# Chunk-selected attention with a gated linear unit: fp16 keys and queries spread by DMA, two gate taps on GpSimd, fewer constants loaded

## The chip, the cores and the metric

The kernel runs on one core of a Trainium2 chip. The metric is device time in microseconds (us) of one execution of the whole kernel. The engines are named as in the profile: PE (TensorE; PEld is its weight load), DVE (VectorE), ACT (ScalarE), POOL (GpSimd) and SP (SyncE, which here issues DMAs). "L793" is line 793 of the kernel before.

## The reference

There are 4 batches with 8 heads, 768 positions and 64 columns per head, all fp32. Keys are cut into 24 chunks of 32 positions. For each query an upper bound of its score with every chunk is formed from the chunk's minimum and maximum; the six chunks with the highest bound are kept, and ordinary causal softmax attention runs on those alone. The result, 512 columns wide, then goes through a gated linear unit: a causal convolution of five taps per column gives a gate, a matmul with `w_val` gives a value, and their product is multiplied with `w_out`.

```
k_min, k_max = min and max of k over each chunk of 32
ub   = sum(maximum(q*k_min, q*k_max))          # future chunks: -1e9
top  = the 6 chunks with the highest ub
attn = softmax(q k^T / 8, only chunks in top, only positions j <= i)
x    = attn v                                  # heads side by side: 512 columns
gate = sigmoid(sum over 5 taps of conv_w[t] * x[s-4+t])
out  = (gate * (x w_val)) w_out
```

## The kernel before

The work is cut into 16 pairs of heads; four pairs (512 columns) make a batch. Everything for a pair has two heads in the upper and lower 64 partitions.

`load` issues the DMAs of a pair's keys, queries and values (`kn`, `qn`, `vn`, positions on partitions) on SP, and for pair 0 on ACT's queue too. `kq(p)` turns keys and queries round with fp32 transposes on PE (L548) into PSUM banks. ACT copies them to SBUF as fp32 (`k32` L559, `q32` L581) and makes the rectified queries `rq` (L586). DVE takes minima and maxima of the chunks (L565). POOL casts each head's half into the fp16 score operands `KE` and `QU` (L573, L592, four casts of 64x384 each), casts values into `VA` (L636), and, from pair 2 on, builds the bound operand `KB` (L607, L614). There are three `KE`/`QU`/`VA` buffers, so pair p writes the buffer that pair p-3 used.

`sel(p)` makes the choice: matmuls of `rq` and `q32` with `KB` (L664) give the bounds, DVE adds a loaded table `cfill` that marks future chunks (L671, into SBUF tile `mub`), takes the eight highest per query (L680), compares with the sixth (L687) and writes the mark `NS`. PE transposes it (L697). For pairs 0 and 1 ACT and DVE copy one head's half each into the spare rows of `QU` (L720); from pair 2 on ACT copies all to `t_m` (L711) and two DMAs on SP carry the halves (L715). Rows of `KE` with a constant -240 per chunk (table `echunk`) make the score matmul itself add the penalty.

`attn(p)` works on 11 banks of scores: score matmuls (L793), the exponential on ACT (L800, `t_P`), a triangular select on POOL where a bank holds diagonal blocks (L807), value matmuls with a column of ones (L824). DVE divides by the sum (L750, L754). A DMA transpose puts the result into `xT`, columns on partitions (L766); the last pair uses PE and ACT (L775, L780).

`moe_gate` makes the gate of a pair's 128 columns in two halves of 384 positions. The first tap, split into two fp16 parts, is a PE matmul with a diagonal (L850); taps 2 to 5 are DVE instructions that add to the PSUM bank (L859). In the last batch the third pair has three taps and the fourth all five on PE. The diagonals are built at the start by DVE (L931). ACT takes a tanh (L863). `moe_val` (L874, L881) and `moe_out` (L890, L896 or L900, output DMA L903) finish a batch.

The order of work on each engine is written by a planner (`class Plan`). Each operation is added with a cost, a due time (`key`, moved by a table `SHIFT` per kind of operation), what it reads and writes, and buffers or PSUM banks that it needs (`CAPS`, `BUFS`). `order` walks through modelled time and picks, for each engine, the ready operation that is due first. Where PE would idle, it puts in warm-up matmuls on a tile of zeros (`filler`, L530). The result is a fixed sequence for each engine's queue, in which an instruction that waits holds back all behind it. `warm_rows` (L507) is a fixed burst of warm-up matmuls at the start.

Of the kernel before, what the change touches and what calls it, by code (L numbers as in the profile page):

```python
# [9 lines left out]
FP = mybir.dt.float32  # L10
# [6 lines left out]
class Op:  # L17
    __slots__ = ("eng", "key", "cost", "fn", "kind", "reads", "writes", "new", "need", "ndep",
                 "outs", "after", "ready", "end", "num", "at")


class Plan:
# [18 lines left out]
    def add(self, eng, key, cost, fn, r=(), w=(), new=(), kind=None, at=0.0):  # L41
# [6 lines left out]
        key = round(key + self.shift.get(eng + ":" + what, 0.0), 4)  # L48
        o.eng, o.key, o.cost, o.fn, o.kind, o.new, o.at = eng, key, cost, fn, kind, new, at
        o.reads, o.writes = tuple(r), tuple(w)  # L50
# [33 lines left out]
    def order(self, bufs, caps, filler):  # L84
# [9 lines left out]
        for o in self.ops:  # L94
            tags.update(o.new)
            for x in set(o.reads + o.writes + tuple(n for n, _ in o.new)):
# [4 lines left out]
        last_pe = {n: [u for u in users[n] if u.eng == "PE"][-1] for n in tags  # L101
                   if tags[n] in caps and n in users}
# [140 lines left out]
        while left:  # L243
# [6 lines left out]
            if e == "PE" and busy(s) < 0.42 and (s > free[e] + 0.12 or o.kind or o.cost < 250):  # L250
                if fill(free[e] if s > free[e] + 0.12 else s):
                    continue
# [43 lines left out]
def kernel(  # L296
# [30 lines left out]
    NBUF = 3  # L327

# [4 lines left out]
    MDMA = 2  # L333
    KBPOOL = True

    PTAPS = {(b, ct): 1 for b in range(B) for ct in range(NCT)}
    PTAPS[B - 1, NCT - 2] = 3
    PTAPS[B - 1, NCT - 1] = 5
    DTAPS = [max(PTAPS[b, ct] for b in range(B)) for ct in range(NCT)]

    ident_np = np.eye(128, dtype=np.float32)
    e_np = np.zeros((64, S), dtype=np.float16)
    for c in range(NCH):
        e_np[c, c * CH:(c + 1) * CH] = PEN
    cfill_np = np.zeros((128, SELT, 2, NCH), dtype=np.float32)
    for it in range(1, NT):
        for p in range(128):
            cfill_np[p, it - 1, :, (it * 128 + p) // CH + 1:] = -1.0e9
    cfill_np = cfill_np.reshape(128, SELT * 2 * NCH)

    ident_dr = nc.inline_tensor(ident_np, name="identc")
    e_dr = nc.inline_tensor(e_np, name="echunk")
    cfill_dr = nc.inline_tensor(cfill_np, name="cfill")
# [3 lines left out]
        "SP:kn": -0.2, "ACTQ:kn": -3.6, "SP:qn": 0.7, "ACTQ:E00": -0.6, "SP:vn": -0.62,  # L357
        "SP:cwn": -4.1, "DVE:KB": -1.2, "POOL:NS": 4.8, "POOL:VA": 1.2, "DVE:diag1": 3.8,
        "DVE:diag": 3.6, "PE:knT": -1.9, "ACT:k32": -2.0, "DVE:kmx": 1.8, "DVE:kmn": 1.6,
        "POOL:KE": -0.8, "DVE:KBh": 2.8, "PE:qnT": -1.88, "ACT:q32": -0.4, "ACT:rq": -0.2,  # L360
        "POOL:QU": -7.4, "DVE:top8": -2.0, "DVE:NS": -4.0, "PE:sT": -0.6, "POOL:kmrr": -1.2,
        "POOL:KBh": -4.6, "PE:s": 0.36, "bank0": 0.67, "ACT:P": 0.15, "POOL:Ptri": 0.3,
        "PE:av": -1.2, "bank1": 0.53, "DVE:rcp": -2.5, "DVE:onat": -1.8, "bank3": -0.2,
        "bank4": -0.06, "bank5": -0.04, "bank6": -0.55, "bank7": 0.1, "bank8": 0.12,
        "bank9": -0.62, "bank10": -0.24, "PE:pg": 1.23, "ACT:m16": -4.6, "PE:pv": 0.4,
        "DVE:gv": -3.4, "PE:po": 0.35, "ACT:osb": 1.5, "PE:xTp": 0.9,
    }
    CAPS = {"w": 5, "s": 4, "av": 2, "spare": 2}
    BUFS = {"kn": 3, "qn": 3, "vn": 3, "P5": 2, "kmx": 2, "kmr": 2,
            "q32": 2, "k32": 2, "rq": 2, "mub": 2, "top8": 2, "onat": 2, "rcp": 2, "osb": 4, "m16": 2}  # L370
# [13 lines left out]
    cfill = cpool.tile([128, SELT * 2 * NCH], FP, tag="cfill")  # L384
# [54 lines left out]
    def load(p, which, key, engs=("SP", "SP"), halves=((0, 1),)):  # L439
        b, h0 = p // NCT, 2 * (p % NCT)  # L440
        src = dict(kn=k, qn=q, vn=v)[which]
        for n, ws in enumerate(halves):
            t0, t1 = 3 * ws[0], 3 * ws[-1] + 3
            for hh in range(2):
# [12 lines left out]
    def constants():  # L457
        dve(-9, 0.2, lambda: nc.vector.memset(junk, 0.0), w=("junk",))
        sp(-9, 64, lambda: nc.scalar.dma_start(out=ident, in_=ident_dr.ap()), w=("ident",),
           eng="ACTQ")  # L460
        load(0, "kn", -8.9, ("SP", "ACTQ"), ((0,), (1,)))
        load(0, "qn", -8.88, ("SP", "ACTQ"), ((0,), (1,)))
        sp(-8.7, 96, lambda: nc.scalar.dma_start(out=KE[0][HP[1], 0, :], in_=e_dr.ap()),
           w=("E00",), eng="ACTQ")
        sp(-8.6, 120, lambda: nc.scalar.dma_start(out=cfill, in_=cfill_dr.ap()), w=("cfill",),
           eng="ACTQ")
# [3 lines left out]
        sp(-8.2, 10, lambda: nc.sync.dma_start(  # L470
            out=cwn, in_=moe_conv_w.rearrange("k (c p) -> (k c) p", p=128)), w=("cwn",))
        load(1, "vn", -8.1)
        for i in range(2):
            dve(-8.8, 0.15, lambda i=i: nc.vector.memset(KB[i], 0.0), w=(("KB", i),))
        for i in range(NBUF):
            dve(-8.7 + i, 0.5, lambda i=i: nc.vector.memset(QU[i][HP[1], 0, :], 0.0),
                w=(("QM", i, 0, 0), ("QM", i, 0, 1)))
            dve(-8.7 + i, 0.5, lambda i=i: nc.vector.memset(QU[i][HP[0], 1, :], 0.0),
                w=(("QM", i, 1, 0), ("QM", i, 1, 1)))
        dve(-8, 0.2, lambda: nc.vector.tensor_copy(out=identh, in_=ident), r=("ident",),  # L480
            w=("identh",))
        for i in range(NBUF):
            for hh in range(2):
                if i or hh:
                    pool(-4 + 1.5 * i, 0.87, lambda i=i, hh=hh: nc.gpsimd.tensor_copy(
                        out=KE[i][HP[1 - hh], hh, :], in_=KE[0][HP[1], 0, :]),
                        r=("E00",), w=(f"E{i}{hh}",))
        for i in range(2):
            pool(-7.5 + i, 0.6, lambda i=i: nc.gpsimd.memset(NS[i], 0.0),
                 w=(("NS", i, 0), ("NS", i, 1)))  # L490
# [3 lines left out]
        dve(-6, 0.1, lambda: nc.vector.memset(xT[:, :, 0:XP], 0.0),  # L494
# [3 lines left out]
    def warm():  # L498
        pe(-10, 512, lambda: spare("warm", 0, 512, True), r=("junk",), w=("warmed",),
           new=new("warm", "spare", [128, 512]))  # L500
        pe(-9.9, 6 * 512, warm_rows, r=("junk", "warm"), w=("warmed2",),
           new=new("warm2", "spare", [128, 512]))

    def warm_rows():

        def half(r, name, n, st=True):
            nc.tensor.matmul(out=T[name][:, 0:n], lhsT=junk[r, n % 128:n % 128 + 128],  # L507
                             rhs=junk[r, 0:n], start=st, stop=True, skip_group_check=True)

        lo, hi = slice(0, 64), slice(64, 128)  # L510
        for _ in range(4):
            half(lo, "warm", 512)
            half(hi, "warm2", 512)
        for _ in range(2):
            spare("warm", 0, 512, True)
        for _ in range(6):
            half(lo, "warm", 128)
            half(hi, "warm2", 128)
        for _ in range(3):
            spare("warm", 0, 128, True)  # L520
            half(lo, "warm", 128)
            half(hi, "warm2", 128)
        for _ in range(3):
            half(lo, "warm", 384)
            half(hi, "warm2", 384)
            half(lo, "warm", 384, False)
            half(hi, "warm2", 384, False)
# [5 lines left out]
    def filler(name, tag):  # L533
        if name in ("warm", "warm2"):
# [4 lines left out]
    def kq(p, key):  # L539
# [3 lines left out]
        def transposes(which, w, k0):  # L543
            name = (which + "T", p, w)
            nw = new(name, "w", [128, HB])
            for tl in range(3):
# [5 lines left out]
                   new=nw if tl == 0 else (), kind="t", at={1: 10.5, 2: 15.0}.get(p, 0.0))  # L552
                plan.also((name,))
            return name, [(name, tl) for tl in range(3)] + [name]

        def khalf(w, k0):
            name, rd = transposes("kn", w, k0)
            sl, cs = slice(w * HB, (w + 1) * HB), slice(w * 12, (w + 1) * 12)
            act(k0, 0.374, lambda: nc.scalar.activation(out=T["k32", p][:, sl], in_=T[name],  # L559
                                                        func=AF.Copy),  # L560
# [451 lines left out]
```

## Time and profile before

| | us |
|---|---|
| median of three runs | 204.06 |
| lowest, highest | 202.61, 204.32 |
| profiled execution | 204.38 |
| its span, first to last instruction | 202.7 |

| engine | busy us | share of span |
|---|---|---|
| PE | 192.2 | 95% |
| DVE | 167.8 | 83% |
| ACT | 158.9 | 78% |
| POOL | 127.8 | 63% |

DMA moved 30.73 MB, 21.27 MB of it read from HBM. Three of the forty slices, from about 20 to 35 us, have a PE clock of 0.5 to 0.7 of full speed; in all others it is 0.9 or more.

The profile has several views. The page gives busy time per engine, the span in 40 slices, DMA queues, the chain of work that ended last (each step followed back to what released it), and groups of instructions: line, engine, operation, output and inputs with shapes, count, busy time, mean ns of one, then the idle time just before them and what ended it. The trace also answers by stretches of time (busy time of each engine in each), by waits (who waited for whom), and in order of time.

### The profile page before, as it was taken

Reading aid. Unit: us, or ns where it says so; the run is one execution under the profiler, and the core shown is the slowest. Engines: PE = TensorE matmul, PEld = TensorE weight load, DVE = VectorE, ACT = ScalarE, POOL = GpSimd, SP = SyncE. Lnnn points to the kernel's source line nnn. Section 1 sums busy time; section 2 is a strip of 40 time slices with the busy share of each in tenths; the row PEclk is TensorE's granted clock in tenths of the full one; section 3 lists DMA queues with packets and bytes.
Section 4 is the critical chain, followed back from the end, with each engine's and each line's share of the span. In section 5 each row is a group of like instructions: output and inputs, shape, how many; then the busy total and the mean of one; then the engine's idle time right before and its main releaser. Section 6 shows DMA issues by size and latency. Waiting matters only on the chain.

```text
span 202.7 us, 6045 instructions
## 1 busy us (share of the span) xinstructions
PE 192.2 (95%) x2140; PEld 153.7 (76%) x2140; DVE 167.8 (83%) x518; ACT 158.9 (78%) x346; POOL 127.8 (63%) x282
## 2 busy tenths in 40 slices
PE   7998489999999999999999999999999999999992
PEld 1556469999986799979897899787989776665550
DVE  5059861977999899999998999999999999988251
ACT  0214368799899999899999999899998989995321
POOL 6647364898978979768867786589676872230000
PEclk9999757999999999999999999999999999999999
DMA  6999994799979699799889687223424112135044
GB/s 140 233 217 218 198 225 73 160 167 212 207 155 176 137 215 204 153 214 192 188 219 225 181 209 175 47 40 98 141 83 128 67 39 54 63 85 207 5 155 155
DMA packets 93277, 30.73 MB, mean 152 GB/s; under 512 B 88138, under 2 KB 90174, under 8 KB 93246
## 3 DMA queue, kind: packets, MB, share of 16 engines
q1 hardware_dynamic: 90222, 28.60, 64.7%
q0 software_dynamic: 1056, 1.05, 3.5%
q10 hardware_dynamic: 1968, 0.68, 1.5%
q8 instruction: 17, 0.28, 0.6%
q14 instruction: 14, 0.11, 0.2%
HBM read 21.27 MB, written 6.29 MB: 136 GB/s over the span
## 4 chain that ended last, share of the span: by engine, by line
PE 85%; ACT 7%; DVE 2%; DMA 2%; issue 1%; POOL 1%; ACTq 0%
PE bank L793 17%; PE bank L664 13%; PE bank L890 10%; PE bank L874 10%; PE bank L548 10%; PE bank L824 10%; PE bank L850 7%; PE bank L530 4%; ACT t_P L800 4%; PE bank L507 2%; PE bank L697 2%; DMA t_vn<-in_v_dram 2%; DVE diag L931 2%; ACT t_k L559 1%; POOL KE L573 1%
## 5 line engine op out<-in xcount | busy, mean ns | idle before, releaser
L800 ACT ACTIVATE t_P<-bank 128x512 f16<-128x512 f32 (+1 forms) x176 | 92.8, 614 | 2.1 <-PE bank L793 1.6
L859 DVE SCALAR_TENSOR_TENSOR bank<-xT,cwT,bank 128x384 f32<-128x384 f16 x116 | 70.9, 616 | 4.3 <-PE bank L850 3.4
L793 PE MATMUL bank<-QU,KE 128*128 128x128 f16 (+4 forms) x448 | 63.4, 252 | 1.3 <-ACT t_P L800 0.8
L592 POOL CAST QU<-t_q 64x384 f16<-64x384 f32 x64 | 32.0, 504 | 24.3 <-PE bank L793 15.6
L793 PEld LDWEIGHTS <-KE 88*128 88x128 f16 (+1 forms) x448 | 37.6, 107 | 8.0 <-issue 1.2
L807 POOL TENSOR_SCALAR_AFFINE_SELECT t_P<-t_P 128x384 f16<-128x384 f16 x64 | 32.9, 524 | 15.0 <-ACT t_P L800 13.2
L573 POOL CAST KE<-t_k 64x384 f16<-64x384 f32 x64 | 32.4, 514 | 8.7 <-ACT t_k L559 5.4
L824 PEld LDWEIGHTS <-t_P 128*128 128x128 f16 x672 | 29.9, 99 | 6.3 <-ACT t_P L800 2.3
L824 PE MATMUL bank<-VA,t_P 128*128 128x65 f16 x672 | 33.9, 193 | 0.4 <-ACT t_P L800 0.4
L664 PEld LDWEIGHTS bank<-KB,t_rq 128*128 128x128 f32 x160 | 27.5, 194 | 2.3 <-ACT t_q L581 0.9
L874 PE MATMUL bank<-xT,wval_sb 128*128 128x384 f16 x128 | 29.0, 326 | 0.0
L890 PE MATMUL bank<-wout_sb,t_gv 128*128 128x512 f16 x96 | 28.4, 379 | 0.0
L664 PE MATMUL bank<-KB,t_rq 128*128 128x48 f32 (+1 forms) x160 | 27.6, 254 | 0.5 <-ACT t_q L581 0.5
L664 PEld LDWEIGHTS bank<-KB,t_q 128*128 128x128 f32 x160 | 27.6, 193 | 0.4
L664 PE MATMUL bank<-KB,t_q 128*128 128x48 f32 (+1 forms) x160 | 27.0, 251 | 0.0
L565 DVE TENSOR_REDUCE t_kmr<-t_k 128x12 f32<-128x384 f32 x32 | 17.4, 545 | 7.7 <-ACT t_k L559 7.7
L559 ACT ACTIVATE t_k<-bank 128x384 f32<-128x384 f32 x32 | 16.5, 516 | 8.1 <-PE bank L548 7.7
L581 ACT ACTIVATE t_q<-bank 128x384 f32<-128x384 f32 x32 | 16.4, 516 | 7.9 <-PE bank L548 7.5
L850 PE MATMUL bank<-xT,diag 128*128 128x384 f16 x88 | 22.3, 326 | 0.0
L863 ACT ACTIVATE t_g<-bank 128x384 f32<-128x384 f32 x32 | 16.5, 518 | 5.0 <-DVE bank L859 2.9
L881 DVE SCALAR_TENSOR_TENSOR t_gv<-t_g,bank 128x384 f16<-128x384 f32 x32 | 17.6, 549 | 2.8 <-PE bank L874 2.4
L896 ACT ACTIVATE t_osb<-bank 128x512 f32<-128x512 f32 x22 | 13.0, 624 | 6.4 <-PE bank L890 5.4
(55 smaller groups left out, 277.6 us busy)
## 6 DMA issues: line engine op xcount, KB each, us to landing
t_vn<-in_v_dram SPq DMA_DIRECT2D x32, 192.0 KB
out_dram<-t_osb SPq DMA_DIRECT2D x24, 256.0 KB
t_kn<-in_k_dram SPq DMA_DIRECT2D x30, 192.0 KB
t_qn<-in_q_dram SPq DMA_DIRECT2D x30, 192.0 KB
QU<-t_m SPq DMA_DIRECT2D x28, 30.0 KB
wval_sb<-in_moe_w_val_dram POOLq DMA_DIRECT2D x1, 512.0 KB, 8.6
wout_sb<-in_moe_w_out_dram POOLq DMA_DIRECT2D x1, 512.0 KB, 7.9
xT<-t_onat SPq DMA_TRANSPOSE x15
```

Source lines behind the costliest of these rows:

```text
L548: lambda tl=tl: nc.tensor.transpose(out=T[name][:, tl * 128:(tl + 1) * 128], in_=T[which, p][:, 3 * w + tl, :], identity=ident),
L573: pool(k0 + (0.6 if p else 2.5), 0.56, lambda hh=hh: nc.gpsimd.tensor_copy(out=ke[HP[hh], hh, sl], in_=T["k32", p][HP[hh], sl]), r=(("k32" ...
L592: pool(k0 + 0.3, 0.56, lambda hh=hh: nc.gpsimd.tensor_copy(out=qu[HP[hh], hh, sl], in_=T["q32", p][HP[hh], sl]), r=(("q32", p, w), ("q32", ...
L664: pe(key, 48, lambda it=it, ts=ts, j=j, x=x: nc.tensor.matmul(out=cols(T[pu][:, it - 1 - i0, :]), lhsT=T[x, p][:, ts], rhs=cols(kb[:, j, : ...
L793: pe(kk, m, lambda hh=hh, c=c, jt=jt, q0=q0, m=m, bank=bank: nc.tensor.matmul(out=T[bank][:, c:c + m], lhsT=ke[KP[hh], hh, jt * 128:(jt + ...
L800: nc.scalar.activation(out=T[pt][:, 0:width], in_=T[bank][:, 0:width], func=AF.Exp, scale=0.125),
L807: nc.gpsimd.affine_select(out=ap, in_=ap, pattern=[[0, tris], [1, 128]], compare_op=ALU.is_ge, fill=0.0, base=0, channel_multiplier=-1)
L824: nc.tensor.matmul(out=T[pav][:, o0:o0 + D + 1], lhsT=T[pt][:, col:col + 128], rhs=va[:, hh, jt, :], start=st, stop=sp_, skip_group_check= ...
L850: nc.tensor.matmul(out=T[pg], lhsT=diag[ct][:, ki, hl, :], rhs=xT[:, slot, X0 + w * HB + ki:X0 + w * HB + ki + HB], start=(n == 0), stop=( ...
L859: dve(kk, 0.525, lambda pg=pg, i=i, c0=c0: nc.vector.scalar_tensor_tensor(out=T[pg], in0=xT[:, slot, c0:c0 + HB], scalar=cwT[:, i:i + 1], ...
L874: pe(key, HB, lambda ct=ct: nc.tensor.matmul(out=T[pv], lhsT=wval_sb[:, ct, et * 128:(et + 1) * 128], rhs=xT[:, slot0 + ct, XP + w * HB:XP ...
L890: pe(key, DM, lambda et=et: nc.tensor.matmul(out=T[po], lhsT=T["gv", b, et][:, s * 128:(s + 1) * 128], rhs=wout_sb[:, et, :], start=(et == ...
```

## The change

- *Keys and queries.* From pair 2 on (`SHUF`), ACT copies the transposed keys straight to fp16 (`k16`), the minima and maxima read the PSUM bank, POOL casts all of `q32` to `q16` and makes `rq` by a maximum with zero, and four DMAs on SP (`spread`) carry the halves to `KE` and `QU`. For pair 0 ACT copies from the bank to `KE` and `QU` directly.
- *Masks.* ACT and DVE copy one half each for every pair; the mask DMAs are gone (`MDMA = 99`).
- *Bounds.* The future mark is added in the PSUM bank, only to the four chunks of the query tile's own columns (40 columns instead of 240); top-8 and comparison read the bank.
- *Gate.* No tap is on PE. ACT writes the first tap to the bank, DVE adds taps 2 and 3, POOL computes taps 4 and 5 over all 768 positions into fp32 tiles and adds them, and DVE adds that sum. The fourth pair of the last batch has no POOL part: DVE does taps 2 to 5.
- *Constants.* `ident`, the chunk rows and the smaller `cfill` are made by POOL with memsets and selects; copies of the rows and memsets of `NS` move from POOL to DVE. `warm_rows` and the diagonals are gone.
- *Last batch.* Three of the four matmuls of each value sum are due before the fourth pair's result (`EARLY`), under a bank limit `v` of four.
- *Loads and planner.* Loads are issued three pairs ahead instead of two; fillers follow other thresholds in the first 36 us; `SHIFT` is rewritten.

```diff
@@ Plan.order
-            if e == "PE" and busy(s) < 0.42 and (s > free[e] + 0.12 or o.kind or o.cost < 250):
+            if e == "PE" and busy(s) < (0.6 if s < 36 else 0.42) and (
+                    s > free[e] + 0.23 if s < 18 else
+                    s > free[e] + 0.12 or o.kind or o.cost < 250):
@@ settings
-    MDMA = 2
+    MDMA = 99
-    PTAPS = {(b, ct): 1 for b in range(B) for ct in range(NCT)}
-    PTAPS[B - 1, NCT - 2] = 3
-    PTAPS[B - 1, NCT - 1] = 5
+    SHUF = 2
+    KDIR = True
+    ENGS = ("SP", "SP")
+    RQP = True
+    PTAPS = {(b, ct): 0 for b in range(B) for ct in range(NCT)}
+    UTAPS = {(b, ct): 2 for b in range(B) for ct in range(NCT)}
+    UTAPS[B - 1, NCT - 1] = 0
-    CAPS = {"w": 5, "s": 4, "av": 2, "spare": 2}
+    CAPS = {"w": 5, "s": 4, "av": 2, "spare": 1, "v": 4}
@@ constants
-        sp(-9, 64, lambda: nc.scalar.dma_start(out=ident, in_=ident_dr.ap()), w=("ident",),
-           eng="ACTQ")
+        def select(t, pattern, op, fill, base, mult):
+            nc.gpsimd.affine_select(out=t, in_=t, pattern=pattern, compare_op=op, fill=fill,
+                                    base=base, channel_multiplier=mult)
+        def identity():
+            nc.gpsimd.memset(ident, 0.0)
+            select(ident, [[-1, 128]], ALU.not_equal, 1.0, 0, 1)
+        def chunk_rows():
+            t = KE[0][HP[1], 0, :]
+            nc.gpsimd.memset(t, PEN)
+            select(t, [[1, S]], ALU.is_ge, 0.0, 0, -CH)
+            select(t, [[-1, S]], ALU.is_ge, 0.0, CH - 1, CH)
+        def future():
+            nc.gpsimd.memset(cfill, 0.0)
+            select(cfill, [[0, SELT], [0, 2], [-CH, 4]], ALU.is_ge, -1.0e9, 0, 1)
@@ kq
+        def spread(src, dst, what, k0):
+            for hh in range(2):
+                sp(k0, 98, lambda hh=hh: nc.sync.dma_start(
+                    out=dst[HP[hh], hh, :], in_=T[src, p][HP[hh], :]),
+                    r=[(src, p)] + [(src, p, w) for w in range(2)],
+                    w=[(what, iN, hh, w) for w in range(2)], rate=240.0)
+            if shuffle and RQP:
+                pool(k0 + 0.1, 0.5 - a / 1000, lambda: nc.gpsimd.tensor_scalar(
+                    out=T["rq", p][:, rsl], in0=T["q32", p][:, rsl], scalar1=0.0, scalar2=None,
+                    op0=ALU.max), r=(("q32", p, w), ("q32", p)), w=(("rq", p, w),),
+                    new=nrq if w == 0 else ())
@@ part
+        def own():
+            x, d = 2 * NCH + 4, 4 * its[0]
+            t = T[pu][:, d:d + n * x].rearrange("p (i x) -> p i x", i=n)
+            return t[:, :, 0:2 * NCH].rearrange("p i (s c) -> p i s c", s=2)[:, :, :, 0:4]
+        dve(key, 0.15, lambda: nc.vector.tensor_tensor(
+            out=own(), in0=own(), in1=cfill[:, 0:n], op=ALU.add),
+            r=[pu, "cfill"] + [(pu, it) for it in its], w=((pu, "own"),))
@@ moe_gate
+        late = KSZ - UTAPS[b, ct]
+            for name, tag, ki in ((u, "u", KSZ - 1), (u2, "u2", KSZ - 2)):
+                i, c0 = ki * NCT + ct, X0 + ki
+                pool(key - 0.1, 0.95, lambda name=name, i=i, c0=c0: nc.gpsimd.tensor_scalar(
+                    out=T[name], in0=xT[:, slot, c0:c0 + S], scalar1=cwT[:, i:i + 1],
+                    scalar2=None, op0=ALU.mult), r=rx + ["cwT"], w=((name, "o"),),
+                    new=new(name, tag, [128, S]))
+            pool(key - 0.1, UCOST, lambda: nc.gpsimd.tensor_tensor(
+                out=T[u], in0=T[u], in1=T[u2], op=ALU.add),
+                r=(u, u2, (u2, "o")), w=((u, "o"),))
+            if taps == 0:
+                act(kk - 0.05, 0.385, lambda w=w, pg=pg: nc.scalar.activation(
+                    out=T[pg], in_=xT[:, slot, X0 + w * HB:X0 + (w + 1) * HB], func=AF.Copy,
+                    scale=cwT[:, ct:ct + 1]), r=rx + ["cwT"], w=((pg, "o"),),
+                    new=new(pg, "w", [128, HB]))
+            if late < KSZ:
+                dve(kk, 0.525, lambda pg=pg, w=w: nc.vector.tensor_tensor(
+                    out=T[pg], in0=T[pg], in1=T[u][:, w * HB:(w + 1) * HB], op=ALU.add),
+                    r=(pg, u, (u, "o")), w=((pg, "o"),))
@@ main loop
-        if p + 2 < NPAIR:
-            for which in ("kn", "qn", "vn"):
-                load(p + 2, which, p - 0.5)
+        if p + 3 < NPAIR:
+            for n, which in enumerate(("kn", "qn", "vn")):
+                load(p + 3, which, p + 0.1 * n, ENGS)
+            moe_val(B - 1, e, w, NPAIR + 0.8 + w + 0.1 * e,
+                    NPAIR - 0.2 + w if e < EARLY else None)
```

In the sequences that the planner writes, the changed kernel has 90 fillers on PE (22 of 512 columns, 68 of 122) where the kernel before has 71 (42 of 512, 3 of 128, 26 of 122) beside the 38 matmuls of `warm_rows`; DVE has 68 gate taps and 30 adds where it had 116 taps; POOL has 4 casts each to `KE` and `QU` where it had 64 each; SP issues 56 spread DMAs where it had 28 mask DMAs. Ten fillers stand ahead of the first key transposes. After the last exponential ACT has 10 output copies, 4 first taps, 5 gates and 2 copies to `xT`; after the last normalisation DVE has 12 taps, 2 adds of POOL's sum, 8 gated products and 2 output copies.

## The prediction

> **What bounds the kernel now.** I read the page's busy shares first, then the stretches of time, then the chain of work that ended last, then groups and waits. Busy shares:
>
> ```profile
> PE 192.2 (95%) x2140; PEld 153.7 (76%) x2140; DVE 167.8 (83%) x518; ACT 158.9 (78%) x346; POOL 127.8 (63%) x282
> ```
>
> PE looks full, but its busy time counts warm-up matmuls and pipelined overlap, so the stretches matter more (columns: length, then busy time of PE, PEld, DVE, ACT, POOL, with instruction counts; then clock, DMA share, GB/s):
>
> ```profile
> 0.00:40.00 40.00, 34.63 (x267) 24.34 (x268) 23.73 (x90) 17.10 (x37) 24.09 (x53) 0.87 1.02 186
> 40.00:176.00 136.00, 134.84 (x1704) 116.34 (x1703) 129.37 (x402) 129.09 (x284) 102.17 (x227) 1.00 0.69 148
> 176.00:202.70 26.70, 22.76 (x175) 13.02 (x173) 14.74 (x28) 12.74 (x27) 1.56 (x3) 1.00 0.33 117
> ```
>
> There are three regimes. In the middle PE lacks 1.2 us of 136, DVE 6.6 and ACT 6.9: PE decides, with two engines close behind. In the first 40 us ACT is idle for 22.9 us: nothing there but a chain of dependences. After 176 us PE decides again. The chain says the same by line, and in order of time it shows the start (start, length, what):
>
> ```profile
> PE 85%; ACT 7%; DVE 2%; DMA 2%; issue 1%; POOL 1%; ACTq 0%
> PE bank L793 17%; PE bank L664 13%; PE bank L890 10%; PE bank L874 10%; PE bank L548 10%; PE bank L824 10%; PE bank L850 7%; PE bank L530 4%; ACT t_P L800 4%; PE bank L507 2%; PE bank L697 2%; DMA t_vn<-in_v_dram 2%; DVE diag L931 2%; ACT t_k L559 1%; POOL KE L573 1%
> ```
> ```profile
> 7.64 2.91 PE bank L530 x13
> 10.55 0.22 PE bank L548 x2
> ...
> 18.73 3.16 DVE diag L931 x11
> ...
> 187.04 1.63 PE bank L850 x10
> ```
>
> The first key transposes (L548) stand at 10.5 us behind warm-up matmuls on PE's queue; diagonals for the gate hold DVE for 3.16 us ahead of the first bounds; near the end ten gate matmuls take 1.63 us, 0.163 each.
>
> **What the Trainium skill says.** "Trace Analysis", Identifying the Most-Contended Engine: matmul busy time is no good measure; agreed here, where a row's mean is 326 ns and its spacing 163 ns. "GPSIMD Engine Reference", 3.1: a two-input add takes 4,497 ns for 2,048 fp32 columns; that gives an estimate of 4,497 x 768/2,048 = 1.69 us for the new add. The trace has only tiny ones (L607 242 ns for 24 columns, L614 267 for 48). "ScalarE: Activation LUTs", What ACT_TABLE_LOAD costs: 186 ns + 0.833 per column, 93 ns more for a per-partition scale, neighbours overlap by about 93. For 384 columns 506 ns against 516 in the trace, so it agrees; the 93 for a scale isn't in the trace. "SBUF — State Buffer", Who interferes with whom: a VectorE instruction with one SBUF input outside 2-port modes does not contend with GpSimd. The new VectorE adds have one PSUM and one SBUF input, so I charge no contention; no run here shows it yet.
>
> **The change part by part.** Durations are from these rows:
>
> ```profile
> L859 DVE SCALAR_TENSOR_TENSOR bank<-xT,cwT,bank 128x384 f32<-128x384 f16 x116 | 70.9, 616 | 4.3 <-PE bank L850 3.4
> L592 POOL CAST QU<-t_q 64x384 f16<-64x384 f32 x64 | 32.0, 504 | 24.3 <-PE bank L793 15.6
> L573 POOL CAST KE<-t_k 64x384 f16<-64x384 f32 x64 | 32.4, 514 | 8.7 <-ACT t_k L559 5.4
> L586 ACT ACTIVATE t_rq<-bank 128x256 f32<-128x256 f32 (+1 forms) x32 | 14.8, 467 | 0.0
> L881 DVE SCALAR_TENSOR_TENSOR t_gv<-t_g,bank 128x384 f16<-128x384 f32 x32 | 17.6, 549 | 2.8 <-PE bank L874 2.4
> L711 ACT COPY t_m<-bank 128x640 f16<-128x640 f16 x14 | 9.9, 707 | 2.4 <-PE bank L697 2.4
> L485 POOL COPY KE<-KE 64x768 f16<-64x768 f16 x5 | 4.1, 823 | 1.3 <-DMA KE<-echunk 1.1
> ```
>
> *PE.* The 88 gate matmuls go: 88 x 0.163 = 14.3 us, 54 of them (8.8) in the middle, 34 (5.5) after 176. The 38 half-array warm-up matmuls go too, all before 40 us. Fillers on bank space go from 71 to 90, but 42 of 512 columns become 22; they stand where PE would idle. Moving three quarters of the last value sums earlier (24 of 32 matmuls, 3.9 us) uses the room.
>
> *ACT.* Added: 32 first taps written to PSUM. Between 0.42 (516 less 0.1 overlap) and 0.51 (with the page's 93 ns); I take 0.47: +15.0. Eight direct key and query copies of pair 0, 0.38 each: +3.0. Fourteen half-masks at 0.57 (L720: 0.667 less overlap): +8.0. Removed: 28 rectified queries at 0.28 and 0.38 (spacing of L586 starts): -9.2; 14 mask copies at 0.61: -8.5. Sum +8.3: 158.9 becomes 167.2.
>
> *DVE.* 116 taps become 68: 48 x 0.611 (70.9/116) = -29.3. Thirty adds of the GpSimd sum, by L881's row 0.55: +16.5. Bound fill 40 columns for 240: 15 x (0.40 - 0.17) = -3.4. Fourteen more half-masks x 0.49 = +6.9. Diagonals -6.9. Pattern copies and memsets taken over from POOL: about +2.5. Minima, maxima and top-8 read PSUM instead of SBUF; no row tells the difference, between -3 and +10 us over 216 instructions, and I take 0. Sum about -14: 154, roughly -9 in the middle.
>
> *POOL.* -61.1 (60 casts each of L573 and L592); fp16 queries 28 x 0.506 = +14.2; rectified queries 14 x (0.50 + 0.40) = +12.6; 30 taps of 768 columns by L485's 0.83 = +24.9; 15 adds x 1.69 = +25.4 (1.0 if the slope of L607 to L614 held); constants about -2. Sum 141.5, some 80% of the stretch in which it has work. In its in-order queue a group of three gate operations (3.3 us) stands before triangular selects (L807), for which diagonal value matmuls wait, then PE's queue. I charge 0 because selects are issued banks ahead of their use; Rival C is that cover gone.
>
> *DMA and SP.* 56 spreads of 96 KB add 5.5 MB, 28 mask DMAs of 30 KB go. In the middle engines were busy 0.69 at 148 GB/s, so 214 GB/s when full; 5.5 MB is 26 us of the 42 that are free. A spread waiting on its row buffer holds back SP's queue: loads, the xT transposes and output. The query casts of before waited 15.6 us for score matmuls to free those same buffers: data is ready over a pair ahead, so a few us of landing time are covered. Value 0, high end 14 x 0.5 = 7.
>
> *PSUM.* Bounds stay in their bank through fill, top-8 and compare (about 1.6 us for 0.4), keys through ACT and two reductions. No row shows a bank wait as such; 0 to 5 us, folded into the middle's idle time.
>
> *The start.* Identity no longer comes by DMA (before, VectorE's cast waited for it to 6.4 us), pair 0's keys and queries are first on both queues, the transposes stand behind 10 fillers rather than some 60 warm-up matmuls, and POOL casts and diagonals leave the chain. First transposes at 5 to 6 us for 10.4; then two half copies, reductions, bounds, top-8, mask and scores, about 8 us when nothing else stands in line: first exponential near 14 us for 26.4. Bank ramp and DMA of later pairs remain, so of 22.9 us idle I keep 15 (between 12 and 19).
>
> *Sum.* ACT is now the fullest engine, so I count along it. The last exponential ends at 181.8 us: 150.7 of work (158.9 less 8.2 after it) and 31.1 idle, 22.9 of it before 40. In the changed order 10 output copies, 4 taps, 5 gates and 2 xT copies follow it, 11.7 us, so 155.5 precede. With 15 idle at the start and 6 later (8.2 before; PE gives room), it ends at 176.5. The tail hangs on DVE: 1.8 to the last normalisation (as now, 181.8 to 183.6), then 12 taps, 2 adds, 8 gated products, 1 output copy, 7.0 + 1.0 + 4.2 + 0.7 = 12.9, then matmuls, copies and landing 5.0 (3.3 from the last copy to the end now): 19.7 for 20.9. Span 196.2. The profiled execution took 204.38 for a span of 202.7, 1.7 around it: 197.9. The median of 204.06 is 0.3 lower: **197.5 us**.
>
> **Rivals.** *A, the whole start is won and ACT runs as PE did, near 99%:* idle 12 + 3, span 190.2, 191.5 us. For it: the slack that PE and DVE get. Against: four engines above 85% together. *B, ACT takes the place of PE with nothing won:* taps at 0.51 (+1.3), 19 idle at the start, 7 later: span 202.5, 203.9 us, no change. For it: ACT was at 95% in the middle. *C, slower: POOL's gate groups delay the selects.* Fifteen groups of 3.3 us in one queue; if each makes PE and then ACT wait 0.9 us more, 15 x 0.9 = 13.5, 211 us; it decides from 6.5/15 = 0.43 us a group on, where the forecast's gain is used up. For it: POOL was already busy for 34.8 of the 40 us from 40 to 80. Against: value matmuls waited for POOL only 0.5 us in all. *That the change does not do what it says:* the spreads' landing late would show as scores waiting on DMA; inside B and C.
>
> **Numbers.** 1% is about what a measurement can tell from no change here, 202.0 to 206.1. Forecast 0.48, A 0.20, B 0.17, C 0.15. Faster: forecast, A, and 0.04 of B, 0.72; same 0.13 (most of B); slower 0.15. The range, 190 to 206, leaves out the lower half of A and most of C.
>
> **What would show it.** Right: first exponential near 14 us; no tap matmuls; ACT the fullest engine, at 97% or more in the middle; last exponential near 177; tail on DVE, 20 us. Wrong: scores waiting on spread DMAs, value matmuls waiting on selects, POOL adds far from 1.7 us, ACT idle more than 8 us in the middle, or a cold clock at the start stretching the ramp.

## The result and the profile after

| | us |
|---|---|
| changed kernel, median of 4 (lowest, highest) | 239.44 (237.75, 242.13) |
| kernel before beside it, median of 4 | 203.34 (201.24, 204.32) |
| ratio, 95% interval | 1.179 (1.164 to 1.194) |
| profiled execution of the changed kernel | 242.13, span 240.4 |

The change makes the kernel 17.9% slower; 239.44 us is 42 us above the forecast and 33 above its range. The profiled execution is the slowest of the four, 1.1% above the median. From here line numbers are those of the changed kernel. Its busy shares, and the stretches (columns as in the prediction, the cuts set where its own regimes change):

```profile
PE 195.3 (81%) x2033; PEld 155.0 (64%) x2033; DVE 161.1 (67%) x501; ACT 170.4 (71%) x359; POOL 199.5 (83%) x263
```
```profile
0.00:40.00 40.00, 34.22 (x354) 27.59 (x354) 26.33 (x101) 27.12 (x60) 26.89 (x57) 1.00 1.09 200
40.00:214.00 174.00, 140.15 (x1499) 115.55 (x1499) 115.51 (x363) 128.40 (x270) 164.22 (x200) 0.89 0.65 136
214.00:240.40 26.40, 20.88 (x180) 11.86 (x180) 19.25 (x39) 14.91 (x30) 8.40 (x8) 0.99 0.36 128
```

GpSimd, the fifth busy column, went from 127.8 us to 199.5 and is the fullest engine. In the long middle it lacks 9.8 us of 174, where PE lacks 33.9, DVE 58.5 and ACT 45.6: before, those three lacked 1.2, 6.6 and 6.9 of 136. Counted along GpSimd, the span is 199.5 of work and idle time of 13.1 in the first 40 us, 9.8 in the middle and 18.0 at the end, 240.4 in all. Such a sum can be made for any engine; that GpSimd sets the pace is what the chain of work that ended last says, which ran over PE for 85% before.

```profile
POOL 56%; PE 24%; ACT 7%; issue 5%; DVE 4%; DMA 2%; ACTq 1%; POOLq 0%
```

The groups of instructions, those that answer to the rows of before (casts, rectified queries, taps, gated products) and the new ones (L927 is ScalarE's first tap, L941 its tanh):

```profile
L901 POOL TENSOR_SCALAR t_u<-xT,cwT 128x768 f32<-128x768 f16 x30 | 66.1, 2210 | 0.8 <-DMA xT<-t_onat 0.8
L906 POOL TENSOR_TENSOR t_u<-t_u,t_u 128x768 f32<-128x768 f32 x15 | 27.2, 1812 | 0.3
L616 POOL TENSOR_SCALAR t_rq<-t_q 128x256 f32<-128x256 f32 (+1 forms) x28 | 28.3, 1010 | 0.8 <-ACT t_q L609 0.7
L860 POOL TENSOR_SCALAR_AFFINE_SELECT t_P<-t_P 128x384 f16<-128x384 f16 x64 | 33.3, 528 | 9.9 <-ACT t_P L853 9.5
L626 POOL CAST t_q<-t_q 128x384 f16<-128x384 f32 x28 | 13.8, 509 | 0.3
L933 DVE SCALAR_TENSOR_TENSOR bank<-xT,cwT,bank 128x384 f32<-128x384 f16 x68 | 41.6, 615 | 4.5 <-ACT bank L927 3.8
L938 DVE TENSOR_TENSOR bank<-bank,t_u 128x384 f32<-128x384 f32 x30 | 16.8, 561 | 7.4 <-POOL t_u L906 7.0
L960 DVE SCALAR_TENSOR_TENSOR t_gv<-t_g,bank 128x384 f16<-128x384 f32 x32 | 17.5, 548 | 3.1 <-PE bank L953 2.4 <-ACT t_q L609 0.2
L927 ACT ACTIVATE bank<-xT,cwT 128x384 f32<-128x384 f16 x32 | 18.9, 590 | 0.3
L941 ACT ACTIVATE t_g<-bank 128x384 f32<-128x384 f32 x32 | 15.9, 497 | 7.3 <-DVE bank L938 6.9
```

The cast of a whole half (L626) costs what one of 64 partitions did, and the adds (L906, L938) are near their estimates. The taps on GpSimd (L901) take 2.21 us where I had put 0.83, the rectified queries (L616) 1.01 on average for 0.45. What that does to the others is in the list of waits (us in total, times, longest):

```profile
DVE t_rcp L803 <- PE bank L877: 29.6, 20, 3.9
PEld L877 <- POOL t_P L860: 26.7, 18, 2.8
ACT t_P L853 <- PE bank L846: 22.9, 21, 3.5
PE bank L877 <- POOL t_P L860: 22.8, 17, 2.5
```

Value matmuls (L877) and their weight loads wait for GpSimd's triangular selects (L860), 26.7 us for the loads where it was 0.5 before. VectorE then waits for the value sums, and ScalarE for scores that stand behind those matmuls on PE's queue. One gate group on GpSimd in order of time (start, length):

```profile
61.01 1.01 POOL L860 TENSOR_SCALAR_AFFINE_SELECT t_P<-t_P 128x384 f16<-128x384 f16 x2
62.01 2.21 POOL L901 TENSOR_SCALAR t_u<-xT,cwT 128x768 f32<-128x768 f16 x1
64.18 0.53 POOL L860 TENSOR_SCALAR_AFFINE_SELECT t_P<-t_P 128x384 f16<-128x384 f16 x1
64.69 2.21 POOL L901 TENSOR_SCALAR t_u<-xT,cwT 128x768 f32<-128x768 f16 x1
66.86 0.53 POOL L860 TENSOR_SCALAR_AFFINE_SELECT t_P<-t_P 128x384 f16<-128x384 f16 x1
67.35 1.81 POOL L906 TENSOR_TENSOR t_u<-t_u,t_u 128x768 f32<-128x768 f32 x1
```

The group is 2.21 + 2.21 + 1.81 = 6.2 us, and the selects are already squeezed between its parts. The start did what was forecast. PE's fillers and first transposes in the chain, and ACT's first exponentials:

```profile
2.92 4.02 PE bank L530 x9
6.94 0.66 PE bank L548 x3
```
```profile
15.54 1.09 ACT L853 ACTIVATE t_P<-bank 128x512 f16<-128x512 f32 x2 [0.75 <-PE bank L846]
```

### The profile page after: what moved, and what is told of

Its sections match the earlier page's. It is cut to its first block, busy times and chain, and to the rows that moved or that the text cites. A ratio compares the mean times of both kernels' runs of the same rounds, so it can differ in the third digit from the quotient of the medians.

```text
span 240.4 us, 5841 instructions
## 1 busy us (share of the span) xinstructions
PE 195.3 (81%) x2033; PEld 155.0 (64%) x2033; DVE 161.1 (67%) x501; ACT 170.4 (71%) x359; POOL 199.5 (83%) x263
## 4 chain that ended last, share of the span: by engine, by line
POOL 56%; PE 24%; ACT 7%; issue 5%; DVE 4%; DMA 2%; ACTq 1%; POOLq 0%
POOL t_u L901 21%; POOL t_P L860 9%; POOL t_rq L616 8%; POOL t_u L906 7%; PE bank L877 5%; PE bank L846 4%; POOL VA L682 4%; PE bank L969 4%; POOL t_q L626 3%; PE bank L714 3%; PE bank L953 3%; ACT t_P L853 3%; PE bank L530 3%; POOL KB L662 2%; ACT t_k L563 1%
## 5 line engine op out<-in xcount | busy, mean ns | idle before, releaser
L853 ACT ACTIVATE t_P<-bank 128x512 f16<-128x512 f32 (+1 forms) x176 | 93.8, 586 | 24.3 <-PE bank L846 22.9
L846 PE MATMUL bank<-QU,KE 88*128 88x128 f16 (+4 forms) x448 | 69.9, 263 | 1.9 <-ACT QU L773 0.8
L901 POOL TENSOR_SCALAR t_u<-xT,cwT 128x768 f32<-128x768 f16 x30 | 66.1, 2210 | 0.8 <-DMA xT<-t_onat 0.8
L877 PE MATMUL bank<-VA,t_P 128*128 128x65 f16 x672 | 31.8, 203 | 23.2 <-POOL t_P L860 22.8
L846 PEld LDWEIGHTS <-KE 88*128 88x128 f16 (+1 forms) x448 | 42.6, 117 | 8.1 <-issue 3.9
L877 PEld LDWEIGHTS <-t_P 128*128 128x128 f16 x672 | 28.2, 105 | 27.9 <-POOL t_P L860 26.7
L933 DVE SCALAR_TENSOR_TENSOR bank<-xT,cwT,bank 128x384 f32<-128x384 f16 x68 | 41.6, 615 | 4.5 <-ACT bank L927 3.8
L860 POOL TENSOR_SCALAR_AFFINE_SELECT t_P<-t_P 128x384 f16<-128x384 f16 x64 | 33.3, 528 | 9.9 <-ACT t_P L853 9.5
L616 POOL TENSOR_SCALAR t_rq<-t_q 128x256 f32<-128x256 f32 (+1 forms) x28 | 28.3, 1010 | 0.8 <-ACT t_q L609 0.7
L803 DVE RECIPROCAL t_rcp<-bank 128x6 f32<-128x6 f32 x32 | 5.9, 191 | 33.3 <-PE bank L877 29.6
L969 PE MATMUL bank<-wout_sb,t_gv 128*128 128x512 f16 x96 | 27.2, 379 | 0.9 <-ACT t_g L941 0.9
L906 POOL TENSOR_TENSOR t_u<-t_u,t_u 128x768 f32<-128x768 f32 x15 | 27.2, 1812 | 0.3
L563 ACT ACTIVATE t_k<-bank 128x384 f16<-128x384 f32 (+1 forms) x32 | 16.0, 500 | 13.8 <-PE bank L548 12.6
L938 DVE TENSOR_TENSOR bank<-bank,t_u 128x384 f32<-128x384 f32 x30 | 16.8, 561 | 7.4 <-POOL t_u L906 7.0
L941 ACT ACTIVATE t_g<-bank 128x384 f32<-128x384 f32 x32 | 15.9, 497 | 7.3 <-DVE bank L938 6.9
L682 POOL CAST VA<-t_vn 128x384 f16<-128x384 f32 x32 | 15.8, 511 | 5.7 <-DMA t_vn<-in_v_dram 3.8
```

What stands on the lines that cost most here:

```text
L616: pool(k0 + 0.1, 0.5 - a / 1000, lambda: nc.gpsimd.tensor_scalar(out=T["rq", p][:, rsl], in0=T["q32", p][:, rsl], scalar1=0.0, scalar2=Non ...
L682: pool(key + (1 if p else 2.5), 0.5, lambda hh=hh: nc.gpsimd.tensor_copy(out=va[:, hh, :, 0:D], in_=T["vn", p][:, :, hh * 64:(hh + 1) * 64 ...
L846: pe(kk, m, lambda hh=hh, c=c, jt=jt, q0=q0, m=m, bank=bank: nc.tensor.matmul(out=T[bank][:, c:c + m], lhsT=ke[KP[hh], hh, jt * 128:(jt + ...
L853: nc.scalar.activation(out=T[pt][:, 0:width], in_=T[bank][:, 0:width], func=AF.Exp, scale=0.125),
L860: nc.gpsimd.affine_select(out=ap, in_=ap, pattern=[[0, tris], [1, 128]], compare_op=ALU.is_ge, fill=0.0, base=0, channel_multiplier=-1)
L877: nc.tensor.matmul(out=T[pav][:, o0:o0 + D + 1], lhsT=T[pt][:, col:col + 128], rhs=va[:, hh, jt, :], start=st, stop=sp_, skip_group_check= ...
```

## Experiments

**The theory:** GpSimd's new work, above all the taps, is so long that the engine sets the pace. **Rivals:** the operation is slow only beside VectorE or with these types; the fixed order is wrong, not the amount of work; some other part of the change costs. All ratios are against the kernel before.

**1. Taps 4 and 5 back on VectorE.** One setting:

```diff
-    UTAPS = {(b, ct): 2 for b in range(B) for ct in range(NCT)}
+    UTAPS = {(b, ct): 0 for b in range(B) for ct in range(NCT)}
```


> The changed kernel, with the two GpSimd taps given back to VectorE: four taps there for every tile, first tap still on ScalarE; the planner makes a new order. Theory: POOL's queue sets the pace of the changed kernel, by 30 taps of 2.21 us and 15 adds of 1.81 us. POOL's busy time falls from 199.5 to about 106 us, DVE's rises from 161 to about 181 us (60 taps more at 0.61, 30 adds of 0.56 fewer), and the time falls to 203 to 213 us with DVE as the fullest engine. Rival one: the rest of the change (spreads on SP, banks held longer, first taps on ScalarE) costs the time; then it stays above 230 us.

212.27 us, ratio 1.050 (1.044 to 1.056). GpSimd falls to 108.5 us and the wait for its selects to a quarter:

```profile
PEld L877 <- POOL t_P L860: 6.3, 13, 1.0
```

With this order, GpSimd taps in place of VectorE's cost 27.2 us of the 239.44, 1.8 us for each of the 15 groups. Some 5% remain.

**2. Rectified queries back on ScalarE, alone and together with 1.**

```diff
-    RQP = True
+    RQP = False
```


> The changed kernel, with only the rectified queries given back to ScalarE (28 instructions); the GpSimd taps stay. Theory: POOL's busy time falls by 28.3 to about 171 us and the time by 15 to 28 us, to 211 to 224 us; POOL stays the fullest engine. Rival one: ScalarE, which gets about 10 us more work, makes it no faster than 236 us.

> The changed kernel without any multiplication or maximum on GpSimd: taps on VectorE, rectified queries on ScalarE. POOL's busy time about 78 us, DVE's about 181, ACT's about 180. Theory: DVE and ACT bound it, 202 to 213 us, no better than with the taps alone taken off. Rival one: above 230 us.

Alone 230.54 us (1.135, 1.120 to 1.149), 8.9 better than the change and less than expected. With the taps away too 215.69 (1.063, 1.052 to 1.073), 3.4 worse than with the taps away alone. So their 28 us on GpSimd cost something while that engine is full and nothing here once it has room. Whether ScalarE is then the worse place isn't shown: with another gate (6) the same move wins 7 us.

**3. The price by itself.** A small kernel of its own that leaves out the whole computation and writes zeros: GpSimd operations in a row on tiles in SBUF, VectorE idle, then two beside VectorE instructions with two SBUF inputs.

> A kernel of its own that leaves out the whole computation and writes zeros: GpSimd instructions of 384 and 768 columns, three of each kind in a row, with VectorE idle. Theory: a GpSimd tensor_scalar is slow by itself, 2.2 us for 768 columns and 1.17 for 384 whatever the types, where a copy takes 0.82 and 0.50. Rival two: it is slow in the changed kernel only because VectorE works beside it; then it takes about 0.82 us for 768 columns here. Rival three: the fp32 output makes it slow; then a copy to fp32 takes about 2.2 us too and a tensor_scalar from fp16 to fp16 about 0.82.

The groups on GpSimd (`s` is a pointer operand; without it, in L56, the operation is a maximum with an immediate; the last row is the one beside VectorE):

```profile
L50 POOL TENSOR_SCALAR o<-a,s 128x768 f32<-128x768 f16 x3 | 6.6, 2201 | 0.0
L52 POOL TENSOR_SCALAR o<-a,s 128x768 f16<-128x768 f16 x3 | 6.6, 2199 | 0.1
L56 POOL TENSOR_SCALAR o<-a 128x768 f32<-128x768 f32 x3 | 6.4, 2126 | 0.3
L60 POOL TENSOR_TENSOR o<-a,b 128x768 f32<-128x768 f32 x3 | 5.4, 1799 | 0.2
L48 POOL CAST o<-a 128x768 f32<-128x768 f16 x3 | 2.5, 820 | 0.0
L69 POOL TENSOR_SCALAR p<-o,s 128x768 f32<-128x768 f32 x2 | 4.7, 2366 | 0.2
```

The operation is slow with nothing beside it, whatever the types and with either kind of scalar. It takes 2.7 times the cast of the same shape and more than an add of two tensors. VectorE with two SBUF inputs beside it adds 7%. So this rival falls for the taps. Other operations can lose more beside VectorE: at the head of this kernel GpSimd's copies and casts of 768 columns took 1.14 to 1.15 us while VectorE copied and cast, and 0.82 after.

**4. One part alone on the kernel before.** Taps 4 and 5 of the 14 tiles that had one tap on PE go to GpSimd, as in the diff of the change, and DVE adds the sum; nothing else.

> The kernel before with nothing but taps 4 and 5 of the 14 tiles that have one tap on TensorE moved to GpSimd, and its sum added by VectorE. Theory, the GpSimd gate alone is enough to make the kernel slower: GpSimd gets 14 x (2 x 2.2 + 1.8) = 87 us on top of 128, 215 in all, so 222 to 245 us with value matmuls waiting for selects. Rival, it hurts only beside the rectified queries and the fp16 casts that the changed kernel also gives to GpSimd: 200 to 215 us.

269.5 us, 1.313 (1.298 to 1.328): the part alone is enough, and costs more than in the change and than I expected. GpSimd has its 128 us and 86 more; the rest is idle time, which I put down to a table of due times made for other work:

```profile
PE 221.9 (83%) x2221; PEld 168.2 (63%) x2221; DVE 157.1 (58%) x490; ACT 161.0 (60%) x346; POOL 214.0 (80%) x324
```

**5. True costs for the planner.** Same operations as the change:

```diff
-    UCOST = 1.75
+    UCOST = 1.78
-                pool(k0 + 0.1, 0.5 - a / 1000, lambda: nc.gpsimd.tensor_scalar(
+                pool(k0 + 0.1, 1.14 - a / 400, lambda: nc.gpsimd.tensor_scalar(
-                pool(key - 0.1, 0.95, lambda name=name, i=i, c0=c0: nc.gpsimd.tensor_scalar(
+                pool(key - 0.1, 2.18, lambda name=name, i=i, c0=c0: nc.gpsimd.tensor_scalar(
```


> The changed kernel with the same instructions, but the planner counts 2.18 us for each GpSimd tap, 1.14 (384 columns) and 0.82 (256) for the rectified queries and 1.78 for the sum, in place of 0.95, 0.5, 0.37 and 1.75. Theory, the amount of work decides: GpSimd still has about 199 us to do, and neither the first 10 us nor the tail hold much of it, so 222 to 240 us. Rival, the fixed order decides, because it was written for operations half as long: 200 to 215 us, with value matmuls hardly waiting for GpSimd's selects.

245.92 us, 1.208 (1.198 to 1.218), a little above what was expected: the order is no better for knowing the costs. Yet the wait that stood out is gone. The selects now come ahead of the gate's work:

```profile
PEld L877 <- POOL t_P L860: 0.4, 1, 0.4
```

The gate's work comes late instead: GpSimd's last two groups run from 218.4 to 230.9 us. So the waits for selects are one form that the excess of GpSimd's work takes, and an order without them gives nothing back. In 10 it has a new table too.

**6. The gate of before in the changed kernel.** What of the remaining 5% is the rest of the change?

```diff
+    PTAPS = {(b, ct): 1 for b in range(B) for ct in range(NCT)}
+    PTAPS[B - 1, NCT - 2] = 3
+    PTAPS[B - 1, NCT - 1] = 5
+    UTAPS = {(b, ct): 0 for b in range(B) for ct in range(NCT)}
```


> The changed kernel with the gate of the kernel before: one tap on TensorE (three and five in the last two pairs of the last batch), the others on VectorE, none on GpSimd or ScalarE. The rectified queries stay on GpSimd, which has some 106 us to do. Theory, all of the loss is the gate and the rest of the change keeps the gain of its start (first exponential near 15.5 us, 10 us earlier than before): 190 to 200 us. Rival, the rest of the change costs by itself what it wins at the start: 201 to 212 us.

> As the run with the gate of the kernel before, with the rectified queries on ScalarE from the PSUM bank too. Theory: ScalarE has some 161 us to do and GpSimd 82; if ScalarE has room now that the first taps are gone, within 2 us of the run with them on GpSimd, or up to 4 us faster where the bounds waited for GpSimd. Rival, ScalarE is the next engine to bind: 4 to 9 us slower than that run.

221.94 us (1.088, 1.078 to 1.099) and, with the queries on ScalarE, 214.63 (1.056, 1.050 to 1.062). The first is slower than either theory said, and the second is faster than the first by more than expected. With 13 us less work on ScalarE than in 1 the kernel of the first is 10 us slower, and 8 us more on ScalarE make the second 7 faster. PE has its 14.3 us of tap matmuls back, but it too is idle for 23 of 217 us; no engine is full. That points to an order that fits badly, which 7 and 9 test.

**7. The start alone.** `SHUF = 99`, `MDMA = 2`, the gate of 6, with the due-time table of before, then with that of the changed kernel.

> The changed kernel with its middle put back: the gate of the kernel before, casts of each head's half on GpSimd for every pair, rectified queries on ScalarE, the mask DMAs from pair 2 on and the due-time table of the kernel before. What is left of the change is the start without loaded constants and warm-up rows, the fill in PSUM, loads three pairs ahead and the early value sums. Theory, the gain at the start is real and nothing else in this remainder costs: 190 to 198 us. Rival, what the start wins the middle gives back: 201 to 207 us.

> The same with the due-time table of the changed kernel. If the 10 us that the changed kernel still lost with its taps on VectorE come from an order written for other operations, this is 205 to 220 us and well above the run with the old table; if they come from the operations themselves, it is within 3 us of that run.

206.04 us (1.021, 1.014 to 1.029) and 214.88 (1.064, 1.054 to 1.074): 9 us between two orders of the same operations. And the gain of the start is lost even with the old table, though the first exponential is at 15.55 us. ACT's exponentials in two stretches show where. Before:

```profile
20.00:40.00 20.00, 5.88 (x11) 0.74 0.89 169
40.00:60.00 20.00, 11.18 (x22) 1.00 0.98 179
```

With the start alone and the old table:

```profile
20.00:40.00 20.00, 10.00 (x19) 0.91 1.05 196
40.00:60.00 20.00, 4.80 (x9) 0.91 1.03 185
```

By 60 us it has done 31 exponentials (3 before 20 us), the kernel before 33. Between 39 and 53.9 us ACT ran none: in its queue stood copies of keys, queries and masks of later pairs, in PE's their transposes and bounds.

**8. Spreads added to 7.** `SHUF = 2`, queries on ScalarE, old table with two entries for the new casts.

> The run with the old table plus one part of the change: from pair 2 on fp16 keys and queries, cast whole and carried to their rows by 56 DMAs, with the rectified queries still on ScalarE. GpSimd has about 82 us to do in place of 128. Theory, the spreads cost nothing, because rows are ready early: within 3 us of the run without them. Rival, 5.5 MB more in a stretch in which the DMA engines are nearly full to 100 us, and SP's queue held by each spread: 4 to 12 us slower than the run without them.

221.31 us (217.50 to 224.22) against 202.63; the executions differ much, but the fastest is still 11 us above the slowest without the spreads (206.39). This alone would speak against the spreads, as one wait on them is now long:

```profile
POOL t_q L630 <- DMA QU<-t_q: 17.7, 8, 9.4
```

GpSimd's next cast waits there for the DMA that still reads its buffer. 9 shows that a kernel with the spreads need not lose that.

**9. New orders for the same operations.** The table `SHIFT` was searched anew for each set of operations, by random changes that were kept where the planner's own end came earlier. Nothing else changes, but for the planner's costs as in 5 (and 0.47 for the first tap). First the gate of before with spreads and queries on GpSimd (6), then the taps on VectorE (1):

> The same operations as the run with the gate of the kernel before (222 us), with a due-time table searched anew for them and the planner told 1.14 us and 0.82 for the rectified queries. Theory, that run lost to its order: 198 to 206 us. Rival, the spreads, the masks or the queries on GpSimd cost by themselves: 212 us or more.

> The same operations as the run with all four late taps on VectorE (212 us), with a due-time table searched anew and the planner told the measured costs of the rectified queries and of ScalarE's first tap. Theory: the 9 us that this run still lost against the kernel before are its order, 199 to 206 us. Rival, VectorE with some 175 us to do is full and decides: 209 us or more.

201.52 us (0.991, 0.986 to 0.995) for 221.94, and 205.25 (1.015, 1.003 to 1.028) for 212.27. The busy shares of the first pair, old table and new:

```profile
PE 193.9 (89%) x2128; PEld 151.2 (70%) x2128; DVE 173.7 (80%) x539; ACT 155.2 (71%) x327; POOL 108.7 (50%) x218
```
```profile
PE 184.9 (92%) x2070; PEld 148.4 (74%) x2070; DVE 172.9 (86%) x539; ACT 154.5 (77%) x327; POOL 108.5 (54%) x218
```

The same counts and times on DVE, ACT and POOL (PE's fillers differ), and 17 us less span: that loss was order. With all late taps on VectorE 1.5% stay, hardly clear of noise; VectorE has 174.6 us to do there and lacks 3.2 of the 96 us from 80 to 176.

**10. A new order for the whole change.**

> All operations of the changed kernel, the planner told the measured costs of GpSimd's and ScalarE's, and a due-time table searched anew for them. Theory, the amount of GpSimd's work decides and no order saves it: GpSimd still has about 199 us to do, 225 to 245 us. Rival, the order was the cause: below 215 us.

239.34 us, 1.184 (1.171 to 1.196), no better than the change. GpSimd has the same work, and value matmuls (L880 here) wait little for its selects:

```profile
PE 194.7 (82%) x2010; PEld 145.9 (61%) x2010; DVE 160.0 (67%) x501; ACT 170.0 (72%) x359; POOL 199.1 (84%) x263
```

```profile
PEld L880 <- POOL t_P L863: 1.9, 3, 1.3
```

From 40 to 220 us it is busy for 165.7 of the 180. As in 5 the gate is late instead: GpSimd's last add ends at 224.1, as at 225.4 in the change. The chain that ended last runs over GpSimd for only 11% here, over PE, DVE, ACT and DMA for most of the rest, so the 199 us are a floor for these operations, and what lies above it is not GpSimd's alone. The search that won 7 and 20 us in 9 wins nothing here. With both orders searched alike, GpSimd taps in place of VectorE's cost 239.34 - 205.25 = 34 us, 2.3 a group.

**11. The start with a new order.** As 7, with the masks of the change (`MDMA = 99`) and a searched table:

```diff
     SHIFT = {
+        "ACT:P": 5.87, "ACT:QM": -5.99, "ACT:g": -1.06, "ACT:k16": -0.73, "ACT:k32": -0.98,
+        "ACT:osb": 1.44, "ACT:pg": 5.84, "ACT:q32": 4.94, "ACT:xT": -2.02, "DVE:NS": 0.07,
... (the other entries of the new table; the old ones go)
     }
```


> The start, the loads, the fill in PSUM, the half-masks on ScalarE and VectorE and the early value sums of the change, with the gate, the casts and the rectified queries of the kernel before, and a due-time table that was searched anew for this set of operations. Only the order of the work is new beside the two runs with the start alone, whose first exponential was at 15.5 us too. Theory, the order lost what the start had won: 193 to 200 us, faster than the kernel before. Rival, the middle is full and no order keeps the gain: 203 us or more.

196.97 us, 0.976 (0.969 to 0.982): 2.4% faster than the kernel before. ACT's exponentials in the same stretches:

```profile
20.00:40.00 20.00, 10.71 (x21) 1.00 1.10 212
40.00:60.00 20.00, 12.88 (x25) 1.00 1.19 195
```

50 of 176 exponentials are done by 60 us for 33 before, and the lead is kept: the last one starts at 165.4 us for 180.6. How much of the 2.4% is the start's and how much the search's isn't shown, because the kernel before was not run with a table searched in the same way.

## Why the prediction was wrong

- **Start: near.** First transposes at 6.7 us (5 to 6), first exponential at 15.5 (14), ACT idle in the first 40 us 12.9 (15, before 22.9).
- **Tail: right in length.** The last exponential ends at 219.7; 20.7 us follow (19.7). VectorE is busy for 14.2 of the next 14.8 us, as forecast. PE counts as busy for all of them and the chain runs over PE, so which of the two holds the end isn't settled.
- **PE, ACT: near.** The tap matmuls are gone; ACT has 170.4 us of work (167.2), its first tap 0.59 each as the profile counts it. That is 0.09 above its tanh of the same size (L941), so the prediction's 93 ns for a per-partition scale show here; the next instruction starts 0.51 us after it (at 218.7, 221.4 and 225.9), the upper end of my 0.42 to 0.51.
- **DVE: near, 161.1 for 154.** Minima and maxima from PSUM take 0.545 to 0.549 us as from SBUF (0.543 to 0.545 before), so the 0 that I took for them holds. Where the other 7 us come from wasn't traced. The adds that read one SBUF tile take 0.561 beside a busy GpSimd against the 0.55 put down for them: no sign of contention, as the Trainium skill has it ("SBUF — State Buffer", Who interferes with whom).
- **POOL: the step that failed.** "30 taps of 768 columns by L485's 0.83 = +24.9" was 66.1 us, and "rectified queries 14 x (0.50 + 0.40) = +12.6" was 28.3. L485 is a copy. I took its row as that of any operation with one input and gave no upper bound, while for the add I bounded both sides. The terms that I showed add up to 141.8 (I wrote 141.5); with 41.2 + 15.7 + 1.8 for the adds that makes 200.5, 1.0 above the 199.5 measured. The Trainium skill did give the adds ("GPSIMD Engine Reference", 3.1): 1.69 us estimated, 1.81 measured.
- **"I charge 0 because selects are issued banks ahead of their use": failed with it.** The cover was for a 3.3 us group in an engine with room. With 6.2 us in a full engine the value matmuls wait. It isn't a cost of its own, though: where the order takes the wait away (5, 10) the time stays.
- **"ACT is now the fullest engine": failed for the same reason.** With 2.21 us a tap POOL's sum is 199.5, longer than the span that I forecast, before any idle time.
- **"6 later", the idle time that I left ACT in the middle, failed by itself.** It rested on PE's room alone and took for granted that the order would use it. Without GpSimd's taps the remainder of the change was still 5% slower than before, most of it order (9); a gain like the forecast one came only with another table, the gate of before and no spreads (11).
- **Rival C named the right engine and queue.** It kept the short group: its 0.9 us a group compares with 1.8 to 2.3 lost for each (1, 10).

PE's granted clock was 0.66 of full speed from 40 to 60 us and 0.68 from 80 to 100. The second stretch follows one in which PE was idle for 5.5 of 20 us, but from 102 to 108 PE was idle for 2.6 of 6 us and kept the full clock to 126. So why it fell stays open. Nothing shows that it decides the time: the fastest of the four executions had a mean clock of 0.93, two slower ones 0.94, and 10 took as long with 0.95.

**Open.** What the kernel before would take with a table searched anew: no run shows it, and every gain over it in 9 and 11 stands under that. Whether the spreads and the queries on GpSimd cost something of their own: 201.52 with them and 196.97 without, both orders searched, but a search may end better in one case than in the other. Why 4 is so much slower than its GpSimd work demands: I read it as order from its idle time, but it wasn't run with a new table. What fills the change's time above GpSimd's 199 us, and whether a better order than those of 5 and 10 exists.

## To carry to other kernels

A price belongs to an operation on an engine, not to its number of inputs: where the trace lacks the row, bound it from the dearer neighbours too, and sum up the receiving engine with that bound. Before moving work to an engine with an in-order queue, ask what else on that queue others wait for. In a kernel with a written order, a set of operations and its due times are one thing: an edit judged with the old order can show 20 us that are not the edit's.

## What the runs showed of the hardware

All durations are for 128 partitions, from the kernel of experiment 3, with VectorE idle where nothing else is said. GpSimd's multiply with a scalar takes 2.20 us for 768 columns, with fp16 or fp32 input alike; its maximum with a constant takes 2.13 for 768 columns of fp32 and 1.16 for 384. Its fp32 add of two tensors takes 1.80 and its fp16 add 1.63, while a cast takes 0.82 and a select 0.83: of these operations with one input, those with a scalar are the dear ones, dearer than two inputs. Beside VectorE instructions with two SBUF inputs the multiply takes 2.37; copies and casts of 768 columns that ran in part beside VectorE's own copies and casts took 1.14 to 1.15 for 0.82. VectorE's minima and maxima take 0.545 to 0.549 us for 384 columns from PSUM in the changed kernel and 0.543 to 0.545 from SBUF in the kernel before.
